# A pool of 33 weight buffers becomes one of 34, and a slot's four weight splits become two and two

## The chip, the core and the metric

The kernel runs on one core of a Trainium2 chip. Five engines work side by side, each through its own list of instructions in order: TensorE (PE, matrix products), VectorE (DVE), ScalarE (ACT), GpSimd (POOL) and SyncE (SP), which issues the transfers between the chip's main memory and the on-chip buffer. An instruction that has to wait holds back all that stands behind it on its engine. The metric is the device time in microseconds (us) of one execution.

## What is computed

Windowed attention, then two layers of dense work on its result:

```python
scores = scale * np.matmul(q, k.transpose(0, 1, 3, 2))      # 4 batches, 8 heads, 576 positions, 64 wide
scores = np.where(mask, scores + bias[None], -1000000000.0) # mask: the last 128 positions
...
x = ...                                # attention out, 2304 tokens x 512
h = x @ w_in                           # 512 -> 2048
g = s * np.maximum(h, 0.0) ** 2 + b
x = g @ w_out                          # 2048 -> 512
a = x @ w1; b = x @ w2                 # 512 -> 1024 each
h = a * b @ w3                         # 1024 -> 1024
out = h @ w_out2                       # 1024 -> 512
```

All is in float32; the weights of the first layer come in a wider form and are decoded on the chip.

## The kernel before

The tokens are cut into six tiles of 384 (`NTILE`, `TT`). The first layer's 2048 hidden columns are cut into 16 chunks (`NC1`). Chunk c of tile t takes three parts: h(t,c), the product with w_in chunk c (`mlp_h`, L501 for tile 0, L510 for the later ones); relu (L521) and square (L526) on ACT; and x(t,c), the product with w_out chunk c (`mlp_x`, L556 for tile 0, L562 later), which adds into four accumulators. Below, h(14) or x(14) alone mean tile 0.

A `slot` holds two chunks (2m and 2m+1) and one attention head of the next tile: scores (L310, L311), a masked minimum on DVE (L324, L333), the exponential (L347) and its norm (L358, L359, L361) on ACT, transposes on PE (L387), their copies (L399, L400), a selection on POOL (L403) and the product with v (L440).

**Decode.** Tile 0 uses each weight chunk as it is decoded, in plain float32. A chunk's raw tile is read by ACT (L102), then DVE takes three steps (L104, L107, L113); the last writes a new tile `wz` of the pool `wp`, and the raw tile is given back. The chunks come in the order wi0, wo0, wi1, wo1 ... wi15, wo15 (w_in and w_out); wi14 is what h(14) waits for, wo14 what x(14) waits for. The two tiles `z` between the steps come from a pool of two, so ACT's L102 of a chunk waits until the chunk before the last has been through L113.

**Split.** Tiles 1 to 5 use each weight as a pair, a rounded part and the rest, so that every product is three passes. `weight_split` takes a new buffer of `wp`, has ACT write the rounded part (L135) and POOL or DVE, in turn, the rest (L136, POOL for the first of a call, DVE for the second), and then the plain tile is given back. `split_some` issues them at the end of a slot, four at a time, from slot m = 6 on: 32 in all. `wp` has 33 buffers. 32 hold weights, and one is spare.

**Later.** When attention is over, its pool `ap` is closed and a pool `lp` takes its place. In the last tile's eight slots the weights w1 and w2 are decoded and split (`w_chunk`, through `w_tick`, L622 to L690), with results in `wp` as far as `free_w` allows. Chunk c = 0 of them has its three pairs in `lp` (tag `wab`, three buffers). Then come `w3_unit` (L597) and the last layers (L832, L871). While attention still runs, `predecode` decodes later weights through one or two tiles `st`: the first from `ap`, the second from `wp` after the splits.

The program order of the Python code gives priorities; a scheduler of the framework, with a timing model of its own, sets each engine's final order. So the order of instructions can move wherever a buffer comes free at another time.

## Time and profile before

| | |
|---|---|
| median of 3 runs | 871.37 us (870.8, 871.37, 878.88) |
| the profiled execution | 871.08 us; its span, first to last instruction, 869.3 us |
| PE busy | 853.8 us, 98% of the span |
| DVE, ACT, POOL busy | 573.2, 494.8, 343.5 us |
| largest groups on PE | L510 185.7 us, L562 126.1 us (and 69.5 us for its low part), L832 107.9 us and 83.6 us |

The profile is one execution. A timeline row gives start, duration, engine, line, operation, output and inputs, and in brackets how long the engine had been idle and what released it. PE's busy time counts pipelined products, so a busy PE can still run at half its clock; the clock that was granted is a column of its own.

### The profile page before, as it was taken

To read this page: it belongs to the slowest core of one execution; us is meant where nothing else is said; L and a number is where in the kernel's file an instruction comes from. 1 tells how busy PE (TensorE), PEld (TensorE's weight loads), DVE (VectorE), ACT (ScalarE), POOL (GpSimd) and SP (SyncE) were. 2 spreads that over 40 slices of the span, in tenths; PEclk is the share of its full clock that TensorE was granted. 3 is DMA by queue.
4 is the path that set the end of the run, shared out by engine and by line. 5 is a ranking of instruction groups with operands and counts; after the bars stand their busy time and mean duration, and the time that the engine had idled before them with its cause. 6 is when DMAs were issued, how large, how long until landed. Compare 5 with 4: busy or idle time off the path is not lost.

```text
span 869.3 us, 13624 instructions
## 1 busy us (share of the span) xinstructions
PE 853.8 (98%) x4676; PEld 775.4 (89%) x4676; DVE 573.2 (66%) x1186; ACT 494.8 (57%) x1180; POOL 343.5 (40%) x361
## 2 busy tenths in 40 slices
PE   8999898999999999999999999999999999999998
PEld 5756565999999999999999999889998999889996
DVE  5978887777788798777863988345544446333233
ACT  6767676877777787777764767334332333223222
POOL 0134545888766676667752201541111011101110
PEclk9999999999999999999999999999999999999999
DMA  9854441212444455445421577832338343620001
GB/s 335 313 165 162 161 146 35 90 56 80 133 131 156 172 168 197 152 163 167 164 98 66 182 275 280 299 133 91 128 110 308 125 162 133 236 91 1 1 1 74
DMA packets 51621, 129.10 MB, mean 149 GB/s; under 512 B 5984, under 2 KB 21600, under 8 KB 51552
## 3 DMA queue, kind: packets, MB, share of 16 engines
q1 hardware_dynamic: 51552, 128.23, 42.9%
q8 instruction: 37, 0.61, 0.3%
q14 instruction: 32, 0.26, 0.1%
HBM read 95.70 MB, written 32.51 MB: 147 GB/s over the span
## 4 chain that ended last, share of the span: by engine, by line
PE 76%; DVE 10%; ACT 5%; issue 3%; DMA 3%; POOL 2%; SPq 0%; DVEq 0%; ACTq 0%; POOLq 0%
PE acc L562 14%; PE hp L510 14%; PE oacc L871 12%; PE d L832 12%; PE u L832 9%; PE w3a L597 5%; PE pv L440 3%; PE acc L556 2%; PE hp L501 2%; DMA wr<-w 1%; PE s L310 1%; PE s L311 1%; POOL w L136 1%; PE tp L387 1%; DVE z L107 1%
## 5 line engine op out<-in xcount | busy, mean ns | idle before, releaser
L510 PE MATMUL hp<-x,w 128*128 128x384 f32 x960 | 185.7, 339 | 0.3 <-DVE pp L400 0.2
L510 PEld LDWEIGHTS hp<-x,w 128*128 128x128 f32 x960 | 167.3, 188 | 0.8 <-DVE pp L400 0.5
L562 PE MATMUL acc<-gh,w 128*128 128x384 f32 x640 | 126.1, 339 | 0.4 <-ACT gh L531 0.4
L928 POOL TENSOR_TENSOR p<-mc 128x384 f32<-128x384 f32 (+2 forms) x30 | 30.9, 1037 | 233.7 <-DVE mc L923 220.6
L562 PEld LDWEIGHTS acc<-gh,w 128*128 128x128 f32 x640 | 109.0, 188 | 1.2 <-ACT gh L531 0.8
L832 PE MATMUL d<-xb,wblk 128*128 128x384 f32 x576 | 107.9, 335 | 0.0
L832 PEld LDWEIGHTS d<-xb,wblk 128*128 128x128 f32 x576 | 101.2, 188 | 2.0
L403 POOL TENSOR_SCALAR_AFFINE_SELECT pt<-pp 128x768 fp32r<-128x768 f32 x80 | 77.9, 996 | 35.0 <-DVE pp L400 17.9
L871 PE MATMUL oacc<-w3o,ph 128*128 128x512 f32 x270 | 84.8, 395 | 0.0
L832 PE MATMUL u<-xb,wblk 128*128 128x384 f32 x432 | 83.6, 335 | 0.0
L272 POOL TENSOR_TENSOR kb<-qkraw,ka 128x512 fp32r<-128x512 f32 x40 | 58.5, 1462 | 50.1 <-ACT ka L271 49.7
L832 PEld LDWEIGHTS u<-xb,wblk 128*128 128x128 f32 x432 | 75.6, 188 | 0.9 <-ACT mc L840 0.6
L324 DVE CUSTOM_DVE_ANT_0 ns<-s,relm_sb 128x256 f32<-128x256 f32 (+1 forms) x144 | 52.8, 412 | 28.0 <-PE s L311 21.2
L368 POOL TENSOR_SCALAR pr<-pr,sm 128x128 f32<-128x128 f32 x90 | 46.1, 528 | 63.0 <-ACT z L150 22.8
L562 PE MATMUL acc<-gl,w 128*128 128x384 f32 x320 | 69.5, 337 | 0.7 <-DVE gl L539 0.7
L919 DVE TENSOR_TENSOR mc<-d,mc 128x384 f32<-128x384 f32 x24 | 13.4, 557 | 76.3 <-PE d L832 76.3
L539 DVE TENSOR_TENSOR gl<-r,gh 128x384 fp32r<-128x384 f32 x80 | 55.9, 698 | 8.6 <-ACT gh L531 7.5
L871 PEld LDWEIGHTS oacc<-w3o,ph 128*128 128x128 f32 x270 | 50.4, 188 | 10.4
L840 ACT ACTIVATE mc<-d 128x384 f32<-128x384 f32 x48 | 23.6, 492 | 63.1 <-PE d L832 63.0
L347 ACT ACTIVATE pr<-pr,mn 128x128 f32<-128x128 f32 x120 | 46.8, 392 | 21.4 <-DVE pr L333 21.3
L562 PEld LDWEIGHTS acc<-gl,w 128*128 128x128 f32 x320 | 56.5, 188 | 1.0 <-DVE gl L539 1.0
L521 ACT ACTIVATE r<-hp 128x384 f32<-128x384 f32 x96 | 46.3, 483 | 18.3 <-PE hp L510 13.2
(127 smaller groups left out, 1674.6 us busy)
## 6 DMA issues: line engine op xcount, KB each, us to landing
qkraw<-qk SPq DMA_DIRECT2D x40, 448.0 KB, 3.3
late<-st SPq DMA_DIRECT2D x23, 512.0 KB, 3.5
w<-late SPq DMA_DIRECT2D x23, 512.0 KB, 5.8
raw<-w_in SPq DMA_DIRECT2D x16, 512.0 KB, 6.0
raw<-w_out SPq DMA_DIRECT2D x16, 512.0 KB, 5.8
wr<-w SPq DMA_DIRECT2D x16, 512.0 KB, 4.5
st<-w3T SPq DMA_DIRECT2D x15, 512.0 KB, 3.6
xs<-x2d SPq DMA_DIRECT2D x32, 192.0 KB, 2.6
```

Source lines behind the costliest of these rows:

```text
L272: nc.gpsimd.tensor_tensor(out=kl, in0=k_r, in1=k.bitcast(F32), op=ALU.subtract)
L324: nc.vector.tensor_tensor_reduce(out=n[:, i, cs], in0=dst[i][:, cs], in1=relm_sb[:, VARIANT.get(t * NB + i, 0), cs], scale=2.0 ** -(h + 1) ...
L347: nc.scalar.activation(out=e[:, i, :], in_=e[:, i, :], func=AF.Exp, scale=-1.0, bias=mn[:, i:i + 1], accum_out=sm[:, i:i + 1],)
L368: nc.gpsimd.tensor_scalar(out=e[:, i, :], in0=e[:, i, :], scalar1=sm[:, i:i + 1], scalar2=1.0, op0=ALU.mult, op1=ALU.mult,)
L403: nc.gpsimd.affine_select(out=o[:, :, :, e, :], in_=pp.bitcast(F32), pattern=[[0, 2], [0, NB], [sign, P]], compare_op=op, fill=0.0, base=0 ...
L510: nc.tensor.matmul(out=hp, lhsT=wi[c][:, l, k * P:(k + 1) * P], rhs=xT[t, k][:, r, :], start=(n == 0), stop=(n == 3 * KD - 1),)
L521: nc.scalar.activation(out=rt[:, :TT], in_=hps.pop((t, c)), func=AF.Relu)
L539: nc.vector.tensor_tensor(out=gl, in0=rt[:, :TT], in1=gh.bitcast(F32), op=ALU.subtract)
L562: nc.tensor.matmul(out=x2acc[m], lhsT=wo[c][:, l, ms], rhs=g[r], start=(c == 0 and n == 0), stop=(c == NC1 - 1 and n == 2),)
L597: nc.tensor.matmul(out=accs[i], lhsT=w3g[i // 4, j][:, l, i % 4 * P:(i % 4 + 1) * P], rhs=wo2s[j][:, r, :], start=(j == 0 and n == 0), sto ...
L832: tc.keep_in_program_order(nc.tensor.matmul(out=dst, lhsT=w[:, l, ks], rhs=xblk[bnm, k][:, r, :], start=(start and n == 0), stop=(n == 5), ...
L871: tc.keep_in_program_order(nc.tensor.matmul(out=oacc[t, i], lhsT=p[l][:, cs], rhs=w3o[c][:, r, :], start=(c == 0 and n == 0), stop=(c == N ...
```

## The change

`wp` gets one buffer more, 34, so two are spare while 32 hold weights. Its memory comes from the pool of attention, where the tile `st` stood; the first `st` is now taken from `wp` too. The four splits at a slot's end become two in its middle (behind the exponential, ahead of the decode of that half) and two at its end. In the later stage the first chunk of w1 and w2 keeps two of its pairs in `lp` instead of three; the third goes to `wp`, and `free_w` starts at 2 instead of 1.

```diff
-    wp = ctx.enter_context(tc.tile_pool(name="wp", bufs=2 * NC1 + 1))
+    wp = ctx.enter_context(tc.tile_pool(name="wp", bufs=2 * NC1 + 2))
...
         for names, src in ((("A11", "A12"), z1), (("S1", "S2"), sv[:, :DM]), (("S3", "S4"), sv[:, DM:])):
-            yield 1 if c else 0
-            if c:
+            home = c == 0 and names[0] != "S3"
+            yield 0 if home else 1
+            if home:
+                t = lp.tile([P, 2, DM], F32R, tag="wab", name="wblk", bufs=2)
+            else:
                 t = take_w()
-            else:
-                t = lp.tile([P, 2, DM], F32R, tag="wab", name="wblk", bufs=3)
...
         if mlp:
+            split_some(2 if m >= 6 else 0)
             tick(dec)
...
         if mlp:
-            split_some(4 if m >= 6 else 0)
+            split_some(2 if m >= 6 else 0)
...
         if n == LEAD + NC1 - 1:
-            pres.append([ap.tile([P, 2 * DM], F32, tag="st", name="st"), None])
+            pres.append([wp.tile([P, 2 * DM], F32, tag="w", name="st"), None])
...
-    free_w[0] = 1
+    free_w[0] = 2
```

The scheduler's order moves in two stretches of the program: around the last chunks of tile 0 and the splits, and in the last tile's slots, where w1 and w2 are decoded.

**PE, the last chunks of tile 0.** Names: `hp` is the result of h, `acc` that of x, `s` scores, `tp` transposes. Before, from x(12) and x(13) (the first row, eight products) to h(15):

```order
L556 MATMUL acc<-r,wz 128x386 x8
L501 MATMUL hp<-xe,wz 128x384 x4
L310 MATMUL s_1433<-ka,qa 128x256
L311 MATMUL s_1433<-kb,qa 128x256
L310 MATMUL s_1433<-ka,qa 128x256
L311 MATMUL s_1433<-kb,qa 128x256
L310 MATMUL s_1434<-ka,qa 128x256
L311 MATMUL s_1434<-kb,qa 128x256
L387 MATMUL tp<-ident,pr 128x128 x3
L556 MATMUL acc<-r,wz 128x386 x4
L501 MATMUL hp<-xe,wz 128x384 x4
```

The same place after:

```order
L556 MATMUL acc<-r,wz 128x386 x4
L501 MATMUL hp<-xe,wz 128x384 x4
L310 MATMUL s_1433<-ka,qa 128x256
L311 MATMUL s_1433<-kb,qa 128x256
L310 MATMUL s_1433<-ka,qa 128x256
L311 MATMUL s_1433<-kb,qa 128x256
L310 MATMUL s_1434<-ka,qa 128x256
L311 MATMUL s_1434<-kb,qa 128x256
L556 MATMUL acc<-r,wz 128x386 x4
L387 MATMUL tp<-ident,pr 128x128 x3
L556 MATMUL acc<-r,wz 128x386 x4
L501 MATMUL hp<-xe,wz 128x384 x4
```

x(13) moved from ahead of h(14) to behind the scores; x(14) still stands ahead of h(15).

**ACT, relu and square of chunk 14** (`r_1448`, from `hp_1428`; raw_169, 170 and 171 are wo14, wi15 and wo15). Before:

```order
L102 ACTIVATE z_1375<-raw_169 128x512
L102 ACTIVATE z_1408<-raw_170 128x512
L135 ACTIVATE w_1414<-wz_259 128x512
L135 ACTIVATE w_1417<-wz_294 128x512
L135 ACTIVATE w_1420<-wz_301 128x512
L521 ACTIVATE r_1448<-hp_1428 128x384
L271 ACTIVATE ka_1564<-qkraw_1536 128x512
L256 ACTIVATE qa_1561<-qkraw_1536 128x384
L526 ACTIVATE r_1448<-r_1448 128x384
```

After:

```order
L102 ACTIVATE z_1414<-raw_170 128x512
L135 ACTIVATE w_1420<-wz_301 128x512
L135 ACTIVATE w_1423<-wz_341 128x512
L521 ACTIVATE r_1448<-hp_1428 128x384
L135 ACTIVATE w_1477<-wz_391 128x512
L135 ACTIVATE w_1480<-wz_398 128x512
L102 ACTIVATE z_1487<-raw_171 128x512
L271 ACTIVATE ka_1564<-qkraw_1536 128x512
L526 ACTIVATE r_1448<-r_1448 128x384
```

Three splits stood ahead of the pair L521, L526; now two stand ahead of it and two, with the L102 of wo15, within it. The first two splits of all (`wz_259`, `wz_294`) now stand earlier, ahead of the relu of chunk 12.

**ACT, relu and square of chunk 15.** Before (`r_1497`):

```order
L358 ACTIVATE sm_1473<-sm_1473,warm_174 128x3
L361 ACTIVATE pr_1454<-pr_1454,sm_1473 128x128 x3
L135 ACTIVATE w_1524<-wz_391 128x512
L521 ACTIVATE r_1497<-hp_1487 128x384
L526 ACTIVATE r_1497<-r_1497 128x384
```

After (`r_1503`):

```order
L361 ACTIVATE pr_1454<-pr_1454,sm_1473 128x128 x3
L135 ACTIVATE w_1530<-wz_438 128x512
L135 ACTIVATE w_1533<-wz_445 128x512
L135 ACTIVATE w_1616<-wz_495 128x512
L521 ACTIVATE r_1503<-hp_1493 128x384
L135 ACTIVATE w_1619<-wz_629 128x512
L286 ACTIVATE vv_1505<-vraw_1313 128x4x2x64
L471 ACTIVATE cs_1520<-pv_1511 64x384
L526 ACTIVATE r_1503<-r_1503 128x384
```

One split stood between the norm (L361) and the square; now four stand there, and two attention steps.

## Rows read from the trace of the kernel before

**Rows 1.** The page: the span of the profiled execution.
```profile
span 869.3 us, 13624 instructions
```
**Rows 2.** Busy time by stretch: PE, PEld, DVE, ACT, POOL (instructions), granted clock, DMA.
```profile
132.99:147.06 14.07, 10.63 (x44) 7.17 (x43) 9.18 (x20) 9.40 (x24) 6.05 (x6) 0.88 0.11 34
147.06:158.04 10.98, 10.82 (x63) 9.38 (x62) 9.30 (x22) 9.73 (x24) 10.12 (x11) 1.00 0.46 138
158.04:220.00 61.96, 61.87 (x387) 61.48 (x386) 48.29 (x95) 49.31 (x125) 51.75 (x53) 1.00 0.19 59
```
**Rows 3.** Timeline of PE, x(12) and x(13) to the first x of tile 1.
```profile
125.33 5.40 PE L556 MATMUL acc<-r,wz 128*128 128x386 f32 x16
130.60 2.85 PE L501 MATMUL hp<-xe,wz 128*128 128x384 f32 x8
...
137.92 4.55 PE L556 MATMUL acc<-r,wz 128*128 128x386 f32 x8 [3.44 <-ACT r L526]
142.31 2.76 PE L501 MATMUL hp<-xe,wz 128*128 128x384 f32 x8
...
147.06 2.75 PE L556 MATMUL acc<-r,wz 128*128 128x386 f32 x8
...
158.04 1.63 PE L562 MATMUL acc<-gh,w 128*128 128x384 f32 x8
```
**Rows 4.** Timeline of ACT: the first splits, relu and square of 14, the norm.
```profile
131.97 0.63 ACT L135 ACTIVATE w<-wz 128x512 fp32r<-128x512 f32 x1 [0.70 <-DVE wz L113]
133.99 0.63 ACT L135 ACTIVATE w<-wz 128x512 fp32r<-128x512 f32 x1 [1.39 <-POOL w L136]
135.38 0.63 ACT L135 ACTIVATE w<-wz 128x512 fp32r<-128x512 f32 x1 [0.76 <-DVE w L136]
136.04 0.49 ACT L521 ACTIVATE r<-hp 128x384 f32<-128x384 f32 x1
...
137.36 0.51 ACT L526 ACTIVATE r<-r 128x384 f32<-128x384 f32 x1
...
142.63 0.99 ACT L361 ACTIVATE pr<-pr,sm 128x128 f32<-128x128 f32 x3 [1.96 <-DVE sm L359]
```
**Rows 5.** Timeline of DVE: decode steps of wi13, wi14 and wi15, and attention's minimum.
```profile
118.97 1.38 DVE L113 SCALAR_TENSOR_TENSOR wz<-raw,z 128x512 uint32<-128x512 uint32 x1
120.38 0.43 DVE L324 CUSTOM_DVE_ANT_0 ns<-s,relm_sb 128x256 f32<-128x256 f32 x1
...
121.53 0.56 DVE L333 TENSOR_TENSOR pr<-ns 128x384 f32<-128x384 f32 x1
...
125.01 0.42 DVE L104 TENSOR_SCALAR z<-z 128x512 uint32<-128x512 uint32 x1
...
129.87 0.68 DVE L113 SCALAR_TENSOR_TENSOR wz<-raw,z 128x512 uint32<-128x512 uint32 x1
...
136.42 1.35 DVE L333 TENSOR_TENSOR pr<-ns 128x384 f32<-128x384 f32 x1
...
141.48 0.69 DVE L113 SCALAR_TENSOR_TENSOR wz<-raw,z 128x512 uint32<-128x512 uint32 x1
```
**Rows 6.** Timeline of POOL beside the first of those DVE rows.
```profile
118.36 1.43 POOL L484 TENSOR_TENSOR x<-xf,x 128x384 fp32r<-128x384 f32 x1
119.76 1.72 POOL L272 TENSOR_TENSOR kb<-qkraw,ka 128x512 fp32r<-128x512 f32 x1
```
**Rows 7.** Line L136, the split's second half: count, duration in ns (least/median/most).
```profile
L136 POOL TENSOR_TENSOR w<-wz,w x16: 1271/1298/1612, 132.7 to 215.8; 128x512 fp32r<-128x512 f32 x16
L136 DVE TENSOR_TENSOR w<-wz,w x16: 673/813/1427, 134.7 to 218.1; 128x512 fp32r<-128x512 f32 x16
```
**Rows 8.** Busy time by stretch, as rows 2: the products of x(14).
```profile
137.90:142.30 4.40, 4.38 (x8) 2.34 (x9) 4.33 (x7) 2.77 (x10) 1.00 (x1) 0.61 0.35 108
```
**Rows 9.** Timeline of PE, the two waits where w1 and w2 are decoded.
```profile
494.13 0.96 PE L562 MATMUL acc<-gl,w 128*128 128x384 f32 x4 [0.72 <-DVE gl L539]
...
522.44 1.66 PE L562 MATMUL acc<-gh,w 128*128 128x384 f32 x8 [0.45 <-ACT gh L531]
```

## The prediction, made before the changed kernel had run

> **What bounds the kernel now.** I read the page first, for the span of 869.3 us [rows 1]; the same execution's time is 871.08 us, so 1.8 us lie around the span, and the median of the runs, 871.37 us, is 0.3 us from it. All sums below are made against 871.08. Then I read busy time by stretch [rows 2]: from 158.04 us on PE is busy 61.87 of 61.96 us at full clock, so from there PE itself is the limit and nothing that another engine does better can shorten the time. Between 132.99 and 147.06 it is not: 10.63 us of 14.07, at a clock of 0.88. The timeline of PE [rows 3] says where. PE waits 3.44 us before x(14), for the square L526 on ACT. The eight products of x(14) then take 4.55 us, where those of x(15) take 2.75, since the granted clock falls: it is 0.61 in those 4.4 us [rows 8], a mean of its two levels, 1.00 (2.4 GHz) and half of that. h(15) starts at 142.31, x(15) at 147.06, the first x of tile 1 at 158.04. In a later stretch, where w1 and w2 are decoded, PE waits 0.72 and 0.45 us [rows 9]; I found no other wait of weight behind 158 us.
>
> The timeline of ACT [rows 4] says why x(14) is late: three splits, each waiting for the buffer that the one before gives back (0.70, 1.39 and 0.76 us), stand ahead of the relu at 136.04 and the square at 137.36. h(14) had been through long before: it starts at 130.60 and takes 2.85 us [rows 3]. The timeline of DVE [rows 5] gives a second bound that the wait hides. h(14) starts as the decode of wi14 ends (129.87 + 0.68 = 130.55), and h(15) as that of wi15 ends (141.48 + 0.69 = 142.17). So x(14)'s slow clock cost nothing here: h(15) could not have started earlier.
>
> **What the change removes.** With two spares, the first two splits wait for no buffer. They move up to about 118 us. x(13), about 2.65 us of PE work (half of 5.40 [rows 3]), moves behind the scores, into the time in which PE waited. That alone is a gain only if wi14, wo14 and wi15 are decoded earlier and the squares come earlier. So I follow that chain, with the durations of rows 4 and 5: L104 0.42, L107 and L113 0.69, L333 and its like 0.56, three L324 and their reads 1.05, L136 on DVE 0.68 [rows 7], three L361 0.99. ACT's other steps take 0.5 to 0.6 each.
>
> **The chain, first without any disturbance between DVE and POOL.**
> - wi13 is decoded at 118.97 + 1.38 = 120.35, as before [rows 5]. Behind it DVE now does L136 0.68, L104, three L324, L107, L257, L333, L113 (wo13), L104, L400, L107, L113 (wi14): 6.8 us. wi14 is ready at 127.2; PE is free for h(14) at 128.0, as x(12) now stands alone ahead of it. Before: 130.6.
> - wo14: DVE's L472 has to wait for ACT, where the norm (three L361, 0.99), L526 of chunk 13 and L471 stand in a row behind the reciprocal; then L472, L104, L107, L113. In all 4.6 us, to 131.8.
> - The fourth split's buffer is the one that the raw tile of wo14 gives back, so it waits for this L113. Behind it on ACT stand L521, two more splits (the sixth waits for DVE's L136 of the fourth), L102, L271 and L526: 3.8 us, so the square of 14 lands at 135.6.
> - wi15: behind wo14 DVE has the fourth split's L136, three L324, the sixth's L136, L333, L104, L107, L257, L113: 5.8 us, to 137.6. PE, with x(14) from 135.6, is free for h(15) at 138.3.
> - x(15): from wi15's end the chain is L104, L400, L359, three L361, three splits (the third waits for DVE's L136 of the second), L521, one split, L286, L471 and L526: 7.3 us, to 144.9. Before, x(15) came 147.06 - 142.17 = 4.9 us behind wi15, with one split in this place. That is the price of the change: four splits and two attention steps where one split stood, 2.4 us more.
>
> Against 147.06 this would be a gain of 2.2 us. Nothing hides it or gives it back: the stretch up to 158.04 has PE busy 10.82 of 10.98 us, and after it PE is the limit.
>
> **What disturbs it.** The row on L113 at 118.97 took 1.38 us and not 0.69 [rows 5]. It ends 0.6 us after POOL's L484 ends (119.76), and POOL's next instruction, L272 at 119.76, takes 1.72 where POOL's L136 of the same size takes 1.28 [rows 6, 7]. The two engines took turns. L324 at 120.38, with L272 running beside it, took 0.43, like its kin. L333 takes 0.56 at 121.53 and 1.35 at 136.42, L136 on DVE 0.67 to 1.43 [rows 5, 7]. So a POOL instruction beside such a DVE step holds it back by 0 to the POOL instruction's whole length, 1.28; the two pairs seen add 0.69 and 0.79, 0.74 in the middle. Before, POOL had no split before 132.7 us [rows 7]. Now it has one at about 120, two at 132 to 136, one at 144, and on the chain above I count six meetings: L136 of the second split with POOL's first, wi14's L113 with the selection L403, wo14's L113 with POOL's L136 of the third, the sixth's L136 with that of the fifth, L333 with L272, the eighth's L136 with that of the seventh. Six at 0.74 are 4.4 us; at nothing, 0; at 1.28, 7.7.
>
> The Trainium skill, page "SBUF — State Buffer", section "Who interferes with whom", speaks against the change here: it says that VectorE and GpSimd share one pair of ports, that it is an exclusive lock, and that whichever starts second is blocked for the whole instruction. The rows agree that L113 starts late and then takes its normal time, and they show turns being taken. By that rule in full the six would cost 7.7 us, an estimate from rows 7, and x(15) would start at 152.6.
>
> I take 0.70 each, 4.2 us, near the pairs seen and a little under their middle, since a meeting in which PE or ACT is later still costs less. x(15) then starts at 144.9 + 4.2 = 149.1, 2.0 us later than before, though x(14) is at about the same place and h(15) up to one us earlier.
>
> **The other edits.** The first `st` in `wp`: it is taken when all splits are over, with two buffers spare, and only one pair of transfers on SP changes place; nothing. `wab` with two buffers, the third pair in `wp`, `free_w` 2: one buffer more, one more used. In that stretch L622 of the first pair goes behind the others and PE's products change places in groups. Both waits (1.17 us together [rows 9]) can vanish, or as much can be added: DVE's and ACT's work is the same, and PE's order still has products of h ahead of each x. I take 0, from -1.2 to +1.2.
>
> **Sum.** 871.08 + 2.0 + 0 = 873.1 us.
>
> **Rivals.**
> - Faster: DVE and POOL do not meet on the chain, or where they meet something else is later. Then x(15) starts at 144.9, 2.2 us early: 868.9, or 867.7 if the two later waits vanish too. For it: the median of DVE's L136 is 0.81, only 0.14 over its least [rows 7]. Against: the meetings here follow from splits that start on both engines within 0.6 us. It decides at six meetings of less than 0.36 us each.
> - No effect: the chain's gain and the meetings cancel (0.3 to 0.45 each), PE's start of tile 1 stays within 0.5 us: 871.1. For it: the chain without disturbance is worth 2.2 us, close to half of what the meetings cost.
> - Slower by more: PE's waits, now three (before h(14), x(14) and x(15)), grow and the clock falls for x(15), as it fell behind the 3.44 us wait: 4.55 - 2.75 = 1.8 us more, with no decode behind it to hide it. With meetings at 1.0 (1.8 us more as well) this gives 876.7. It decides where the wait before x(15) comes near the 3.44 us after which the clock fell; in the forecast it is about 2.
>
> **How the numbers follow.** The forecast (x(15) 0.6 to 4 us later, 871.7 to 875.2): 0.58. Faster (under 870.5): 0.22. No effect (870.5 to 871.7): 0.12. Slower by more: 0.08. A range of 868.0 to 875.5 leaves out the last and the far end of the second, about 0.15 in all; the forecast's own is 871.7 to 875.2. One per cent, 8.7 us, is about what a measurement of this kernel tells from no change; no case reaches it, and only what I have overlooked could. Faster by over 1% 0.02, within 0.95, slower 0.03.
>
> **What would show it right or wrong.** In the timeline of PE: x(13) behind the scores, h(14) at 128 to 130, x(14) near 138, h(15) at 141 to 142, x(15) at 149, the first x of tile 1 about 2 us later than 158.04, and PE dense behind that. In that of ACT: the fourth split waiting for L113, and the relu of 15 behind three splits. In that of DVE: L136 and L113 of 1.1 us and more beside POOL's L136. It is wrong if x(15) starts before 147.06, or if PE waits again behind 158 us (splits now come closer together on ACT there), or if the stretch of w1 and w2 moves by more than 1.2 us.

## The result, and the profile of the changed kernel

The changed kernel takes 878.1 us (median of 18 runs). The kernel before took 873.45 in as many runs beside it, so the two are compared by their ratio: 1.0055, interval 1.0037 to 1.0074, or 4.8 us slower (3.2 to 6.5). The forecast was 2.0 us slower, 1.0023; 878.1 lies above its range. The sign was right, the size was not. Three of these runs of the changed kernel and four of the kernel before took 889 us and more, a slow state of the chip, and are left out of the ratio.

The profiled execution took 877.48 us, its span [rows 1]:

```profile
span 875.7 us, 13633 instructions
```

That is 6.4 us over the span of before, 1.6 us more than the ratio says. A profile is one execution: before's, 871.08 us, lies near the fast end of its runs (870.8 at the least), the changed kernel's in the middle of its own (874.94 at the least).

The timeline of PE in the changed kernel, h(14) to the first x of tile 1, and the waits behind it (start, length, engine, line, operation, tiles; in brackets the idle time and who ended it) [rows 3]:

```profile
129.00 2.78 PE L501 MATMUL hp<-xe,wz 128*128 128x384 f32 x8
...
132.33 2.75 PE L556 MATMUL acc<-r,wz 128*128 128x386 f32 x8
...
137.98 4.55 PE L556 MATMUL acc<-r,wz 128*128 128x386 f32 x8 [2.57 <-ACT r L526]
142.37 2.74 PE L501 MATMUL hp<-xe,wz 128*128 128x384 f32 x8
...
149.27 4.49 PE L556 MATMUL acc<-r,wz 128*128 128x386 f32 x8 [1.58 <-ACT r L526]
...
161.57 1.63 PE L562 MATMUL acc<-gh,w 128*128 128x384 f32 x8
...
176.62 2.37 PE L510 MATMUL hp<-x,w 128*128 128x384 f32 x12 [0.33 <-ACT r L521]
...
188.33 2.35 PE L510 MATMUL hp<-x,w 128*128 128x384 f32 x12 [0.77 <-ACT r L521]
...
193.74 0.97 PE L562 MATMUL acc<-gl,w 128*128 128x384 f32 x4 [0.40 <-DVE gl L539]
...
500.46 0.95 PE L562 MATMUL acc<-gl,w 128*128 128x384 f32 x4 [0.91 <-DVE gl L539]
...
519.78 1.66 PE L562 MATMUL acc<-gh,w 128*128 128x384 f32 x8 [0.50 <-ACT gh L531]
```

x(13) stands behind the scores and h(14) at 129.00, as forecast. x(15) starts at 149.27 (147.06 before), its products take 4.49 us (2.75 before), and behind 158 us, where before had no such wait, there are three.

Busy time by stretch, in the order PE, PEld, DVE, ACT, POOL (instructions), granted clock, DMA [rows 2]. First x(15)'s products, then tile 1's first 63 us:

```profile
149.20:153.80 4.60, 4.53 (x10) 2.56 (x11) 4.44 (x10) 4.12 (x13) 4.60 (x6) 0.63 0.13 41
...
161.57:225.00 63.43, 61.88 (x383) 60.49 (x382) 49.31 (x94) 46.71 (x119) 48.60 (x54) 1.00 0.23 73
```

The clock of 0.63 is a mean of 1.00 and one half of it (2.4 and 1.2 GHz). In the second stretch PE is idle for 1.55 us, where before it was idle for 0.09 [rows 2].

The 6.4 us of span are made of four pieces, cut at three starts: x(15), the first x of tile 1, and the relu of chunk 0 of tile 2 (236.38 us before, 242.08 after):

| stretch | before | after | difference |
|---|---|---|---|
| start to x(15) | 147.06 | 149.27 | +2.21 |
| x(15) to the first x of tile 1 | 10.98 | 12.30 | +1.32 |
| from there to relu(2,0) | 78.34 | 80.51 | +2.17 |
| relu(2,0) to the end | 632.9 | 633.6 | +0.7 |

ACT, as [rows 4]: the steps on the way to x(15), and two of the places behind 158 us:

```profile
134.26 0.63 ACT L135 ACTIVATE w<-wz 128x512 fp32r<-128x512 f32 x1 [2.26 <-DVE wz L113]
134.92 0.49 ACT L521 ACTIVATE r<-hp 128x384 f32<-128x384 f32 x1
...
137.43 0.51 ACT L526 ACTIVATE r<-r 128x384 f32<-128x384 f32 x1
...
146.12 0.63 ACT L135 ACTIVATE w<-wz 128x512 fp32r<-128x512 f32 x1 [1.42 <-DVE w L136]
146.66 0.47 ACT L521 ACTIVATE r<-hp 128x384 f32<-128x384 f32 x1
...
148.70 0.52 ACT L526 ACTIVATE r<-r 128x384 f32<-128x384 f32 x1
...
175.56 0.63 ACT L135 ACTIVATE w<-wz 128x512 fp32r<-128x512 f32 x1 [1.42 <-DVE w L136]
176.10 0.47 ACT L521 ACTIVATE r<-hp 128x384 f32<-128x384 f32 x1
...
187.13 0.63 ACT L135 ACTIVATE w<-wz 128x512 fp32r<-128x512 f32 x1 [1.05 <-DVE w L136]
187.78 0.49 ACT L521 ACTIVATE r<-hp 128x384 f32<-128x384 f32 x1
```

The reader is to see one pattern three times, at 146, 175 and 187 us: a split (L135) stands idle for the low half (L136) of an earlier one, and the relu (L521) that PE needs stands behind it in ACT's queue.

The kernel before has the same pattern behind 158 us, and PE doesn't wait. Chunk 6 of tile 1 in before, its h on PE and its relu on ACT:

```profile
177.78 2.27 PE L510 MATMUL hp<-x,w 128*128 128x384 f32 x12
```

```profile
181.44 0.63 ACT L135 ACTIVATE w<-wz 128x512 fp32r<-128x512 f32 x1 [1.05 <-DVE w L136]
182.10 0.49 ACT L521 ACTIVATE r<-hp 128x384 f32<-128x384 f32 x1
```

The last products of the same h in the changed kernel, whose relu is the one at 187.78 above:

```profile
183.22 1.22 PE L510 MATMUL hp<-x,w 128*128 128x384 f32 x6
```

The idle time of the last split is 1.05 us in both. But before, the relu starts 2.1 us after its h has ended (180.05 to 182.10), in the changed kernel 3.3 us (184.44 to 187.78). PE has other products for the time between, and before they last, even at chunk 9, where the relu is 3.15 us behind. In the changed kernel they run out. What differs is how many splits stand between two relus: mostly two and at most three before, three or four at the chunks 3 to 6 after.

DVE in the changed kernel, as [rows 5]: the six steps that meet POOL:

```profile
120.56 1.76 DVE L136 TENSOR_TENSOR w<-wz,w 128x512 fp32r<-128x512 f32 x1
...
127.72 1.16 DVE L113 SCALAR_TENSOR_TENSOR wz<-raw,z 128x512 uint32<-128x512 uint32 x1
...
132.59 1.64 DVE L113 SCALAR_TENSOR_TENSOR wz<-raw,z 128x512 uint32<-128x512 uint32 x1
...
136.56 1.26 DVE L136 TENSOR_TENSOR w<-wz,w 128x512 fp32r<-128x512 f32 x1
137.75 1.62 DVE L333 TENSOR_TENSOR pr<-ns 128x384 f32<-128x384 f32 x1
...
144.74 1.35 DVE L136 TENSOR_TENSOR w<-wz,w 128x512 fp32r<-128x512 f32 x1 [0.72 <-ACT w L135]
```

POOL beside them, as [rows 6]:

```profile
120.05 1.73 POOL L136 TENSOR_TENSOR w<-wz,w 128x512 fp32r<-128x512 f32 x1
...
132.08 1.60 POOL L136 TENSOR_TENSOR w<-wz,w 128x512 fp32r<-128x512 f32 x1 [2.47 <-ACT w L135]
136.00 1.27 POOL L136 TENSOR_TENSOR w<-wz,w 128x512 fp32r<-128x512 f32 x1 [2.32 <-ACT w L135]
137.60 1.35 POOL L272 TENSOR_TENSOR kb<-qkraw,ka 128x512 fp32r<-128x512 f32 x1 [0.32 <-ACT ka L271]
...
144.26 1.28 POOL L136 TENSOR_TENSOR w<-wz,w 128x512 fp32r<-128x512 f32 x1 [5.31 <-ACT w L135]
```

The low halves as a line, as [rows 7] (count, least/median/most in ns, first and last start):

```profile
L136 POOL TENSOR_TENSOR w<-wz,w x16: 1272/1375/1737, 120.1 to 189.0; 128x512 fp32r<-128x512 f32 x16
L136 DVE TENSOR_TENSOR w<-wz,w x16: 660/1194/1762, 120.6 to 191.1; 128x512 fp32r<-128x512 f32 x16
```

The last one starts at 191 us, where before it started at 218, and the median one on DVE takes 1.19 us instead of 0.81.

### The profile page after: what moved, and what is told of

It reads as the page before. It is cut to its first block, busy times and chain, and to the rows that moved or that the text cites. A ratio compares the mean times of both kernels' runs of the same rounds, so it can differ in the third digit from the quotient of the medians.

```text
span 875.7 us, 13633 instructions
## 1 busy us (share of the span) xinstructions
PE 858.0 (98%) x4674; PEld 776.9 (89%) x4676; DVE 578.0 (66%) x1186; ACT 493.8 (56%) x1180; POOL 343.7 (39%) x361
## 4 chain that ended last, share of the span: by engine, by line
PE 74%; DVE 10%; ACT 7%; issue 5%; DMA 3%; POOL 1%; SPq 0%; DVEq 0%; POOLq 0%; ACTq 0%
PE acc L562 13%; PE hp L510 13%; PE oacc L872 12%; PE d L833 11%; PE u L833 9%; PE w3a L597 5%; PE pv L440 2%; PE acc L556 2%; PE hp L501 2%; DMA wr<-w 1%; DVE wz L113 1%; DVE ns L324 1%; PE s L310 1%; DVE w L136 1%; DVE qa L257 1%
## 5 line engine op out<-in xcount | busy, mean ns | idle before, releaser
L510 PE MATMUL hp<-x,w 128*128 128x384 f32 x960 | 186.0, 339 | 1.2 <-ACT r L521 1.1
L510 PEld LDWEIGHTS hp<-x,w 128*128 128x128 f32 x960 | 167.1, 188 | 2.1 <-ACT r L521 2.1
L403 POOL TENSOR_SCALAR_AFFINE_SELECT pt<-pp 128x768 fp32r<-128x768 f32 x80 | 78.1, 999 | 36.0 <-DVE pp L400 22.5
L272 POOL TENSOR_TENSOR kb<-qkraw,ka 128x512 fp32r<-128x512 f32 x40 | 57.4, 1436 | 57.0 <-ACT ka L271 56.4
L521 ACT ACTIVATE r<-hp 128x384 f32<-128x384 f32 x96 | 46.4, 483 | 31.8 <-PE hp L510 25.9
L539 DVE TENSOR_TENSOR gl<-r,gh 128x384 fp32r<-128x384 f32 x80 | 57.7, 721 | 9.0 <-ACT gh L531 7.9
```

What stands on the lines that cost most here:

```text
L272: nc.gpsimd.tensor_tensor(out=kl, in0=k_r, in1=k.bitcast(F32), op=ALU.subtract)
L403: nc.gpsimd.affine_select(out=o[:, :, :, e, :], in_=pp.bitcast(F32), pattern=[[0, 2], [0, NB], [sign, P]], compare_op=op, fill=0.0, base=0 ...
L510: nc.tensor.matmul(out=hp, lhsT=wi[c][:, l, k * P:(k + 1) * P], rhs=xT[t, k][:, r, :], start=(n == 0), stop=(n == 3 * KD - 1),)
L521: nc.scalar.activation(out=rt[:, :TT], in_=hps.pop((t, c)), func=AF.Relu)
L539: nc.vector.tensor_tensor(out=gl, in0=rt[:, :TT], in1=gh.bitcast(F32), op=ALU.subtract)
```

## The experiments

Three theories were tested, for the two places of loss. **A**: splits that find a free buffer move up on ACT ahead of relu and square, and PE waits for these. **B**: what counts is the place of the call, two splits in the middle of a slot and two at its end. **C**: what counts are the turns that DVE and POOL take, since POOL makes half of the low halves.

The table gives, from each profile, x(15)'s start, the time from x(15) to the first x of tile 1, the time from there to relu(2,0), and the ratio to the kernel before. 10.5 and 78.0 us are the least that the last two stretches take in any kernel here. In the executions marked * the first products of the program ran at half speed for a while, long before any split. Their x(15) is given less the delay that this left at the first relu of the MLP, against the changed kernel (3 to 20 us). The others differ there by up to 0.9 us, which is not taken off; before's first relu comes 0.4 us later than the changed kernel's.

| kernel | x(15) | to tile 1 | to relu(2,0) | ratio (interval) |
|---|---|---|---|---|
| before | 147.06 | 10.98 | 78.34 | 1 |
| changed | 149.27 | 12.30 | 80.51 | 1.0055 (1.0037 to 1.0074) |
| e1, 34 buffers, four at the end | 146.76 | 12.68 | 81.72 | 1.0023 (0.9995 to 1.0050) |
| e2, 33 buffers, two and two | 152.71 | 11.62 | 77.96 | 1.0053 (1.0026 to 1.0081) |
| e3, changed, from slot 7 | 146.06* | 12.30 | 82.30 | 1.0016 (0.9985 to 1.0047) |
| e7, changed, L135 in program order | 151.58 | 10.55 | 77.93 | 1.0010 (0.9979 to 1.0042) |
| e5, changed, low halves on DVE | 144.96 | 14.36 | 78.01 | 1.0004 (0.9971 to 1.0037) |
| e6, changed, low halves on POOL | 147.13* | 11.99 | 82.59 | 1.0045 (1.0010 to 1.0080) |
| e8, before, L135 in program order | 147.69* | 10.54 | 77.96 | 0.9978 (0.9952 to 1.0005) |
| e17, e8 again | 149.53 | 10.54 | 77.96 | 1.0009 (0.9983 to 1.0035) |
| e9, e1, L135 in program order | 145.87 | 10.64 | 80.98 | 0.9989 (0.9966 to 1.0012) |
| e10, e7 with low halves on DVE | 148.10* | 11.57 | 78.00 | 0.9999 (0.9976 to 1.0022) |
| e11, e9 with low halves on DVE | 145.26 | 12.08 | 77.97 | 1.0000 (0.9962 to 1.0037) |
| e12, before, low halves on DVE | 148.61 | 11.93 | 80.78 | 1.0045 (1.0017 to 1.0073) |
| e13, e8 with low halves on DVE | 146.20* | 10.70 | 79.10 | 1.0005 (0.9981 to 1.0029) |
| e14, changed, first ten low halves on DVE | 144.70* | 12.42 | 82.12 | 1.0050 (1.0027 to 1.0073) |
| e15, changed, later 22 low halves on DVE | 149.46* | 12.08 | 83.14 | 1.0069 (1.0053 to 1.0086) |
| e16, changed, later 22 L135 in program order | 149.64 | 12.36 | 77.96 | 1.0026 (1.0014 to 1.0039) |

One profile places x(15) only to about 1.8 us (e8 and e17 are one kernel, 147.69 and 149.53), though the three of the changed kernel agree to 0.5.

### The two parts of the change apart: e1 and e2

e1 is the change without the moved call (the first line stands in the middle of a slot, the others at its end):

```diff
-            split_some(2 if m >= 6 else 0)
...
-            split_some(2 if m >= 6 else 0)
+            split_some(4 if m >= 6 else 0)
```

> The changed kernel with one edit taken back: the four splits of a slot stand together at its end again; the 34 buffers and the rest of the change stay. Theory A (splits that find a free buffer move ahead of relu and square on ACT, wherever the call stands): on ACT four splits stand ahead of the relu of chunk 14 and four around that of chunk 15, so x(15) starts 1 to 3 us later than in the kernel before, PE waits again at 165 to 200 us, and the time is 874 to 877 us against 871.4. Theory B (the place of the call, two and two, does it): like the kernel before, 870.5 to 872.5. Theory C (DVE and POOL holding each other up sets it): the POOL halves come at about 131 us and not at 120, so about one meeting fewer than in the changed kernel, 873 to 876.

e2 is the kernel before with the moved call alone:

```diff
+            split_some(2 if m >= 6 else 0)
...
-            split_some(4 if m >= 6 else 0)
+            split_some(2 if m >= 6 else 0)
```

> The kernel before with one edit of the change: two splits in the middle of a slot and two at its end, with 33 buffers in all. Theory A: with one spare each split waits for the one before, and those waits stand on ACT ahead of relu and square as well; x(15) 1 to 3 us late, but no closer splits at 165 to 200 us, so no waits there: 872 to 875 us. Theory B: all of the loss, 874.5 to 877. Theory C: the first two splits come at about 118 us as in the changed kernel, so the same meetings: 874 to 877.

Each part alone has one of the two losses. With the buffers alone x(15) is not late (A had it 1 to 3 us late), but the stretch to relu(2,0) takes 3.4 us more than before. PE's timeline in e1:

```profile
154.53 4.11 PE L510 MATMUL hp<-x,w 128*128 128x384 f32 x22 [1.71 <-POOL x L484]
...
187.33 2.35 PE L510 MATMUL hp<-x,w 128*128 128x384 f32 x12 [0.85 <-ACT r L521]
```

The second row is the pattern of the changed kernel at 188.33. The first is new: at 154.5 us PE waits for tile 1's x, the attention's own chain. With the placement alone nothing waits behind 160 us, but x(15) is 5.6 us late. PE and then DVE in e2:

```profile
145.42 5.30 PE L501 MATMUL hp<-xe,wz 128*128 128x384 f32 x8 [5.38 <-DVE wz L113]
```

```profile
142.88 0.69 DVE L136 TENSOR_TENSOR w<-wz,w 128x512 fp32r<-128x512 f32 x1 [1.57 <-ACT w L135]
...
144.67 0.69 DVE L113 SCALAR_TENSOR_TENSOR wz<-raw,z 128x512 uint32<-128x512 uint32 x1
```

wi15's decode stands in DVE's queue behind a low half, which waits for its own L135 on ACT. So the placement alone brings a loss ahead of x(15) (B), the buffers alone one behind it (A). But e2 is late by another way than the change: there h(15) starts at 145.42, in the changed kernel at 142.37. The parts don't add: e1's and e2's losses by ratio are 2.0 and 4.6 us, the change's 4.8.

### A later start, and the order on ACT: e3 and e7

e3 lets the splits begin one slot later, at both calls (first edit); e7 holds L135 in program order, so that it can't move up (second):

```diff
-            split_some(2 if m >= 6 else 0)
+            split_some(2 if m >= 7 else 0)
```

```diff
-        nc.scalar.activation(out=w[:, 0, :], in_=z, func=AF.Copy)
+        tc.keep_in_program_order(nc.scalar.activation(out=w[:, 0, :], in_=z, func=AF.Copy))
```

> The changed kernel with the splits started one slot later (m = 7 and not 6), so the first two stand around the middle of slot 7. Theory A: no split ahead of chunk 12 and 13, still two to four around the relu of 14 or 15, and splits just as close at 165 to 200 us: x(15) late by 1 to 3 us, 873 to 877. Theory C: the POOL halves now begin at about 131 us, so wi14 is ready by 127 to 128 and h(14) starts at 128; 871 to 874.

> The changed kernel with one edit: each split's ACT step may not move ahead of what the program has ahead of it on ACT, so none stands between a relu and its square in tile 0, and fewer behind them. The buffers, the places of the calls and both engines' halves stay. Theory A: x(14) and x(15) start 1 to 3 us earlier than in the changed kernel (137.98 and 149.27), PE waits under 1 us in all at 165 to 200, the clock doesn't fall for x(15): 868.5 to 872.5 us. Theory C (DVE and POOL): the meetings stay, so 874 to 877.

e3 brings x(15) back (146.06, where A had it 1 to 3 us late) and makes the stretch behind it worse (82.30), with more splits left for it. e7 takes the waits behind 160 us away wholly (77.93), but x(15) is at 151.58, where A had it 1 to 3 us earlier than in the change. Both are within 0.5% of before, and neither interval tells which is better.

### Which engine makes the low halves: e5, e6, e14 and e15

The edit of e5; e6 has `nc.gpsimd` in its place:

```diff
-            weight_split(*unsplit.pop(0), nc.vector if e % 2 else nc.gpsimd)
+            weight_split(*unsplit.pop(0), nc.vector)
```

> The changed kernel with the low half (L136) of every split on DVE, none on POOL. So POOL has no split to take turns with DVE, and DVE has 32 of them instead of 16, 16 x 0.68 = 11 us more over 118 to 190 us, where it is not full. Theory C (the turns that DVE and POOL take are what makes x(15) late): x(15) starts before 147.5 (149.27 in the changed kernel), wi14 and wo14 are ready 1 us earlier, and the time is 1.5 to 3 us under the changed kernel's, 874.5 to 876.5 at 878.1. Theory B (the place of the call itself: splits stand ahead of relu and square on ACT, and each waits for its low half wherever that is made): x(15) within 1 us of 149.27, time within 1 us of the changed kernel's. Theory A speaks only of the waits at 176 to 194 us: they stay, 2 to 3.5 us, under either.

> The changed kernel with the low half (L136) of every split on POOL, none on DVE. POOL takes 1.28 us for one where DVE takes 0.68, so a pair of splits takes POOL 2.6 us, and it meets DVE's decode steps more often. Theory C: the meetings cost on the chain to x(15) as before or more: x(15) at 150 to 152, time 1 to 3 us over the changed kernel's (879 to 881). Theory B: a split's buffer comes back later by 0.6 us for each that was on DVE, so the third and fourth split on ACT, and relu and square behind them, come 0.6 to 1.2 us later: x(15) 150 to 151, time 0.6 to 2 over. Both agree in the sign; against both is a time that is no longer, which would say that DVE's own share of the splits (0.68 each ahead of its decode) was the cost.

With all on DVE x(15) starts 4.3 us earlier. PE and ACT in e5:

```profile
144.96 2.86 PE L556 MATMUL acc<-r,wz 128*128 128x386 f32 x8
...
154.59 3.67 PE L510 MATMUL hp<-x,w 128*128 128x384 f32 x12 [1.82 <-DVE pp L400]
```

```profile
143.51 0.47 ACT L521 ACTIVATE r<-hp 128x384 f32<-128x384 f32 x1
...
144.40 0.51 ACT L526 ACTIVATE r<-r 128x384 f32<-128x384 f32 x1
```

The relu stands at 143.51 instead of 146.66, 3.2 us earlier. Another 1.1 us comes from the order: here the square L526 stands ahead of L286 and L471, in the changed kernel behind them. So at most 3.2 of the 4.3 us are what C says. The waits behind 160 us are gone as well (78.01), though its expectation had them stay. But tile 1 starts only 2.3 us earlier: PE now waits 1.82 us for L400, the end of the attention's chain, and the clock halves behind that wait (3.67 us for twelve products that take 2.38 in e15).

e6 missed. With all low halves on POOL x(15) is not at 150 or later but at 147.1, 2.1 us earlier than in the change (1.1 of them by the same order of L526), and its ratio, 1.0045, is not over the change's. Seven DVE steps between wi13's decode and x(15) are held back by POOL there, but DVE has no L136 in its queue ahead of the decode. So theory C is too narrow: a low half on DVE costs the chain its own length too, and the mixture of both engines is the worst of the three at x(15).

Then only the first ten splits (e14), and only the later 22 (e15, with `q[1] >= 5`):

```diff
-            weight_split(*unsplit.pop(0), nc.vector if e % 2 else nc.gpsimd)
+            weight_split(*(q := unsplit.pop(0)), nc.vector if e % 2 or q[1] < 5 else nc.gpsimd)
```

> The changed kernel, with the low halves (L136) of only the first ten splits all on DVE; the later 22 alternate as in the change. Theory C1 (the two losses are separate, and the first is what POOL's low halves do on the way to x(15)): x(15) at 144.5 to 146, as with all of them on DVE (144.96), the later waits stay at 1.5 to 3.5 us; time 1.0015 to 1.004 of the kernel before. If the later waits also go, they come from how many splits are left over at 160 us, and the time is 1.000 to 1.0015. If x(15) stays at 148 or later, the gain at x(15) with all on DVE came from elsewhere.

> The changed kernel, with the first ten splits alternating as in the change and the low halves of the later 22 all on DVE. Theory C1: x(15) at 148.5 to 150 as in the changed kernel, and the waits of PE at 160 to 230 us under 0.7 (2.0 there): time 1.7 to 2.5 us under the changed kernel's, 1.0025 to 1.0035. If the waits stay, POOL's low halves are not their cause, the closer packing on ACT is, and the time is 1.0045 to 1.006.

The first half of C1 held: x(15) at 144.70 in e14, at 149.46 in e15. The second fell for e15. With the later ones on DVE the waits are not gone, the stretch takes 83.14 us, and the longest wait is at another place, PE's timeline in e15:

```profile
194.00 1.03 PE L387 MATMUL tp<-ident,pr 128*128 128x128 f32 x3 [2.37 <-POOL pr L368]
```

So the sharing of the first ten low halves with POOL makes x(15) late. Behind 160 us the two groups can't be told apart so simply. Where the first ten are on DVE, the engine of the later ones decides: e14 takes 82.12 us, e5, with the later ones on DVE too, 78.01. Where the first ten are shared, moving the later ones doesn't help (e15). Of the kernels that differ from the change in this engine alone, only e5, with all 32 on DVE, has no waits there. e14's 4.6 us at x(15) hardly show in its ratio. Its stretch to relu(2,0) took 1.6 us more than the change's, which leaves 2.8 us by the profile; five of its twelve runs lie at 874.1 to 875.0, under nearly all of the changed kernel, the others above, and the interval holds 1.0027 as well as 1.0055.

### The waits behind 160 us, and the clock: e16, a2 and a3

e16 is the changed kernel with only the later 22 L135 held in program order; up to x(15) all engines' orders are the changed kernel's.

```diff
-        nc.scalar.activation(out=w[:, 0, :], in_=z, func=AF.Copy)
+        (tc.keep_in_program_order if c >= 5 else lambda i: i)(nc.scalar.activation(out=w[:, 0, :], in_=z, func=AF.Copy))
```

> The changed kernel, with L135 held in program order for the splits behind the first ten alone; up to x(15) every engine has the changed kernel's order. Theory A (the waits at 176 to 194 us are relu and square behind splits that moved up): x(15) at 149.3 as in the change, its products at half clock or not as chance has it, and PE's waits at 160 to 230 us under 0.5 (2.0 in the change): 2.0 us under the changed kernel, 1.0025 to 1.004 of the kernel before. Rival (34 buffers bring such waits in any order): waits of 1.5 us or more stay, 1.0045 to 1.0065.

Busy time by stretch in e16, then its PE at x(15):

```profile
161.57:230.00 68.43, 68.43 (x430) 68.21 (x430) 51.25 (x105) 53.20 (x134) 52.91 (x56) 1.00 0.22 68
```

```profile
149.64 4.56 PE L556 MATMUL acc<-r,wz 128*128 128x386 f32 x8 [1.59 <-ACT r L526]
```

PE has no gap left, x(15) and its half clock stand as they were, and the ratio falls from 1.0055 to 1.0026, as theory A had it. In nearly all of these chunks the relu now starts about 0.1 us or less behind the end of its h. The two ratios come from different comparisons, and their intervals touch; the profile alone gives 2.5 us (80.51 less 77.96), of which 1.55 were idle time of PE.

The changed kernel was profiled twice more:

> The changed kernel itself once more, for a second profiled execution. If the half clock at x(15) belongs to the change, its eight products again take 4.4 to 4.6 us (2.75 at full clock) behind the wait of about 1.6 us; the starts of h(14), h(15) and x(15) agree with the first profile to 0.3 us but for the shift of what lies ahead. If the half clock is chance, they take 2.75 and tile 1 starts at about 160.

> The changed kernel itself, a third profiled execution, read for the same three things: x(15)'s start (149.3 + the shift ahead of it), the clock of its products, and the waits of PE at 176 to 194 us (2.0 in the first profile; 1.7 to 2.3 if they belong to the change).

PE in a2; in a3 the two rows stand at 149.74 and 188.76, with waits of 1.58 and 0.78 us:

```profile
149.66 4.55 PE L556 MATMUL acc<-r,wz 128*128 128x386 f32 x8 [1.59 <-ACT r L526]
...
188.74 2.35 PE L510 MATMUL hp<-x,w 128*128 128x384 f32 x12 [0.78 <-ACT r L521]
```

x(15), its clock and the waits all repeat: in three profiles x(15) starts at 149.3 to 149.7, at half clock, and the late waits stand at the same instructions. PE is idle for 1.5 us in them in each profile; the 2.0 that the expectations name is too high.

### Looking for a better version: e8 to e13, e17

The two remedies, L135 in program order and low halves on DVE, were put on the kernel before, on the buffers alone and on the change; the edits are those shown.

> The kernel before, with L135 held in program order (it can't move up past relu, square or the norm on ACT), four splits at the slot's end, 33 buffers. Theory A (splits that find a free buffer move up ahead of relu and square, and PE then waits): in the kernel before three splits stood ahead of the relu that x(14) waited for, 3.44 us; with the pin the squares of 14 come earlier, x(14) starts before 136.5, x(15) before 147, the time is 0.5 to 2.5 us under the kernel before (0.997 to 0.9995). Theory B (only the place of the call counts): the order is nearly the same, x(15) at 146.5 to 147.5 and the time within 0.7 us. What speaks against both: x(15) later than 148, as the pin can also push splits into a worse place.

> 34 buffers and the moved tiles as in the changed kernel, all four splits at the slot's end as in the kernel before, L135 held in program order. Theory A: the 3.10 us of waits between 160 and 230 us that the buffers alone brought vanish (under 0.5), x(15) stays at 146 to 148, and the time is that of the kernel before or up to 2 us under it (0.9975 to 1.0005), 2 to 3 us under that of the buffers alone. If the waits at 160 to 230 come from the buffer itself and not from the order on ACT, they stay at 2 to 3.5 us and the time is that of the buffers alone (1.002).

> The changed kernel with both remedies at once: every low half (L136) on DVE, and L135 held in program order. If the loss of the change is the two things found so far (meetings of DVE and POOL on the chain to x(15), theory C; splits packed ahead of relu on ACT behind 160 us, theory A) and nothing else, both are gone: x(15) at 145 to 147.5, waits of PE at 160 to 230 us under 0.5, and the time is at or under the kernel before (0.995 to 1.000). If a third cause sits in the placement of two and two (theory B: with the pin and POOL, x(15) came at 151.58), x(15) stays at 149 or later and the time at 1.001 or over.

> 34 buffers, four splits at the slot's end, L135 held in program order, low halves on DVE. Beside the same kernel with POOL's share (x(15) at 145.87, waits of 2.1 us at 160 to 230 us, 0.9989): theory C says that the waits left there are splits on ACT that stand idle for a low half on POOL, so they fall under 0.7 us; x(15) at 144 to 146. A second chain then limits: the attention that makes tile 1's x ended at 154.9 us in the kernel before too (a wait of 0.2 us on L400), so tile 1's first x can't come before 156. Time 0.995 to 0.998. Theory A alone (the order on ACT is all): no change from 0.999.

> The kernel before with nothing but the low halves moved to DVE. There ACT stood idle 16.3 us in all in front of splits, for the low half of the split before. Theory C: this falls under 8 us, the wait of 3.44 us before x(14) shrinks by 1 to 2, x(15) comes at 144.5 to 146.5, and since the attention's chain lets tile 1 start no earlier than about 156.5, the gain is 0.5 to 1.5 us: 0.998 to 0.9995. If DVE's and POOL's meetings matter only where four splits come close together (the change), x(15) stays at 147 +- 0.7 and the time at 1.000; if DVE's 11 us more hold its decode back, x(15) comes later than 148 and the time is over 1.001.

> The kernel before with the low halves on DVE and L135 held in program order. The pin alone gave 0.9978 with an interval of 0.9952 to 1.0005. If both remedies add: x(15) at 144 to 146, no wait at 160 to 230 us, 0.9955 to 0.9975. If they cure the same wait (the one before x(14)), the time is that of the pin alone, 0.997 to 0.9985. If DVE is too full: over 0.9985.

> The kernel before with L135 held in program order, a second time. If the first ratio, 0.9978, holds, it is 0.9965 to 0.999 again: 1 to 3 us faster than before, from PE's waits of 0.34 us or less behind 158 us and the earlier square of 14. If it was chance, 0.9995 to 1.001.

e8's 0.9978 did not repeat (e17: 1.0009). e9 missed theory A's number: 3 us are left in its last stretch, because program order itself puts four splits ahead of the next slot's relu; at 203.53 us in e9 a split right ahead of a relu starts after 2.97 us idle for POOL's L136. With the low halves on DVE as well (e11) that is gone, as expected, but the time is level with before and not 0.995 to 0.998 of it. In e12 the case that its expectation named last came: in the kernel before the low halves on DVE cost 1.0045, with x(15) no earlier and 2.4 us more behind tile 1's start, so they are no remedy by themselves. e10, e11 and e13 are level with before, though e10's x(15), 148.10, is later than the 145 to 147.5 of its expectation. No kernel here was shown to beat it.

## Why the prediction was wrong

**The walk held.** wi14 ready at 128.9, h(14) at 129.00 (forecast 128 to 130), x(14) 137.98 (near 138), h(15) 142.37 (141 to 142, so a little late), x(15) 149.27 (149). The sentence that x(15) comes 2.0 us later measured 2.2, and 2.6 and 2.7 in a2 and a3. This bears out a term of about 2 us; that it agrees to 0.2 us is in part luck, since two profiles of one kernel can lie 1.8 us apart at x(15).

**The six meetings held, with their price.** They are the six DVE rows between wi13's decode and x(15) that take over 1.1 us, each beside a POOL row. Over 0.68 (L136), 0.69 (L113) and 0.56 (L333) they took 1.08, 0.47, 0.95, 0.58, 1.06 and 0.67 us more: 4.8 in all, 0.80 each (forecast 0.70). The rows also give the price of one, which the prediction left between 0 and 1.28. Each of the five DVE steps whose POOL row is shown above starts while that POOL step runs, and ends 0.42 to 0.55 us after it: POOL's L136 ends at 121.78 and DVE's at 122.32, POOL's L136 at 133.68 and DVE's L113 at 134.23. In the kernel before it is the same (POOL's L484 ends at 119.79, DVE's L113 at 120.35 [rows 5, 6]). So here a meeting cost what was left of the POOL step when the DVE step started, less 0.13 or 0.14 us. The Trainium skill, page "SBUF — State Buffer", section "Who interferes with whom", gives the shared ports to whoever starts first for its whole instruction and blocks the other; the trace agrees. The prediction's 7.7 us and x(15) at 152.6 by that rule came from counting POOL's whole length, 1.28, in each meeting, though a part of it was over when the DVE step started.

The undisturbed chain gave x(15) at 144.9; e5 and e14, with no low half on POOL there, had 144.96 and 144.70. This agrees but is no exact proof: in these two DVE still meets POOL's L403 and L272, L526 stands ahead of L286 and L471 on ACT, worth 1.1 us, and DVE has more low halves. e6 says that the sum of meetings is not all that counts.

**First step that failed: from x(15) to tile 1, "Nothing hides it or gives it back".** The prediction said this of a gain at x(15), and let the loss pass on as it was in the same way. The stretch behind it grew by 1.32 us, and two things stand there. One is the clock at x(15). The prediction put it into a rival at 0.08 and let it depend on a wait near 3.44 us. The wait was 1.58, in the forecast's own walk about 2, and the clock halved all the same, in four of five profiles with this order up to x(15) (the changed kernel three times, e16). It cost the eight products 4.49 - 2.75 = 1.74 us. In the fifth, e15, the wait was 1.59 and the products took 2.86, at full clock; so the wait's length does not decide alone.

The other is a second chain, the attention that makes tile 1's x (L400, L484). In e15 the full clock at x(15) gave nothing back: its stretch to tile 1 took 12.08 us, 0.2 less than the changed kernel's, since PE then waited for L400:

```profile
165.20 2.38 PE L510 MATMUL hp<-x,w 128*128 128x384 f32 x12 [1.12 <-DVE pp L400]
```

e15 has its later low halves on DVE, which makes L400, so it doesn't price the clock in the change. In the changed kernel the step to look at is L484 on POOL:

```profile
155.09 1.02 POOL L484 TENSOR_TENSOR x<-xf,x 128x384 fp32r<-128x384 f32 x1
```

It ends at 156.11. The product for which PE waits on L484 in e1 starts here at 156.79, as the ninth of the 30 products of L510 that begin at 155.33. An estimate from these rows: with x(15) at full clock, 1.74 us earlier, PE would have waited 1.1 us there, and tile 1 would have started only about 0.7 us earlier. No run separates the two.

**Second step that failed: "from 158.04 us on … PE itself is the limit".** The profile of before showed PE dense there. But ACT was already late in it: splits stood ahead of the relus and waited for low halves, and at chunks 3 to 13 the relus came 1.07 to 3.15 us after their h, just within the time for which PE had other products. With a second spare the splits begin earlier and the last L135 starts at 189.5 us instead of 217.5, so three or four stand between two relus, and PE runs out of work at chunks 4 and 6 and at 193.74. e16 shows it: the same order up to x(15), no split moved up behind it, no waits, 2.5 us less in the stretch. e5 shows that closeness alone is not enough: its splits are over even earlier, at 181 us, but wait for low halves 2.3 us in all, where the changed kernel's wait 7.3, and PE doesn't wait. The prediction named such waits in its last paragraph as what would make it wrong, and gave them no price and no chance. With the 1.3 and 2.2 us that the two steps measured, its sum would have been 876.6 and not 873.1.

**The rival on the faster side had the second chain in its way.** Its 868.9 needs tile 1 to start 2.2 us earlier, at 155.8. No kernel started it there; the earliest is e9, at 156.51. e5 and e1 have x(15) earlier than before and then wait 1.82 us for L400 and 1.71 for L484. A row of before's PE shows how near this chain lay, and was not read:

```profile
154.89 1.31 PE L510 MATMUL hp<-x,w 128*128 128x384 f32 x6 [0.16 <-DVE pp L400]
```

**Other edits at nothing** [rows 9]: 0.91 and 0.50 us after for 0.72 and 0.45 before, +0.24; relu(2,0) to the end in all +0.7, within the 1.2.

What stays open: why the clock halved at x(15) in four profiles and not in e15; how the 1.32 us up to tile 1 divide between the clock and the attention's chain; and what e14's earlier x(15) is worth, since its runs spread too far to say.

## What to carry to other kernels

A dense stretch of the bounding engine is dense for the order in which others feed it, and doesn't show how late they already are: read how far behind each product the next engine's step comes, and for how long the bounding engine has other work. A change that lets side work run earlier must be followed to where that work now stands together, and each such place needs a price. Before counting an early start as gain, look for the chain that ends next: here it lay 0.16 us behind. And a spare buffer lets a scheduler move a producer up in an in-order queue, where it then stands idle ahead of work that the bounding engine waits for; holding only those steps in program order gave back about half of the loss (1.0055 to 1.0026).

## What the runs showed of the hardware that was not expected

**The clock after a wait is not settled by the wait.** Before h(11) PE waits 2.37 us for L472 in the kernel before and in the changed one, and its products took 2.85 us, at full clock, in the one and 4.26, partly at half, in the other. Before x(14) waits of 2.57 (changed, three times) were followed by half clock, 2.56 (e16), 2.50 (e15) and 2.90 (e17) by full. The three profiles of the changed kernel agree at x(14) and x(15); e15, with the same order up to there, differs at both.

**Half speed at the start, without a mark in the record.** In e14 the first six L305 take nearly twice their time; PE in the changed kernel, then in e14:

```profile
5.76 1.37 PE L305 MATMUL s<-qkraw,qe 64*128 64x128 f32 x6
```

```profile
5.76 2.50 PE L305 MATMUL s<-qkraw,qe 64*128 64x128 f32 x6
```

The record of the granted clock says 1.00 for this stretch, yet the rows show half speed, and all that follows comes 2.95 us later. In e10 the record does show it, 0.50 from 15 to 50 us, and the delay is 20 us. Such a delay stands ahead of all that was changed here, so profiles were compared by stretches and not by their spans.
